# Four more chunks of a linear-attention and mixture-of-experts kernel get their y with features on partitions

## The chip, the cores and the metric

One core of one Trainium2 chip runs the whole program. The metric is device time in microseconds (us); the median of the runs of a kernel counts.

## What is computed

```python
state = f[:, :, t, :, None] * state + einsum('bhd,bhde' of k[t], v[t])   # f = sigmoid(f_logit)
y[:, :, t] = np.einsum('bhd,bhde->bhe', q[:, :, t], state)              # B 4, H 8, S 768, D 48
x = y as 3072 tokens x 384
x = (h * sigmoid(h)) @ w_out          # h = x @ w_in, 384 -> 2048 -> 384
out = one of 8 experts per token      # relu(x @ w1[e]) @ w2[e], 384 -> 1024 -> 384, times its gate
```

## The kernel before, in words

The 3072 tokens are 24 **chunks** of 128, six to a batch row. Each chunk goes through the gated linear attention, its result y goes into the first dense layer, and that layer's result is sorted by expert. All large products are made from pairs of rounded halves (hi and lo of the weights, of x and of the hidden layer), so a dense product is three matmuls. Chunks stand in groups (0 and 1; 2 and 3; 4 to 6; then threes), and a group's x has to be there when the first of its dense steps begins.

**A step** s is one pass of the loop at L1439. It makes a hidden piece `ph` of 128 features for one group (`moe_h`: nine matmuls, then tanh into `se` on ACT and the product `sg` on DVE), splits the piece into `gh` (ACT) and `gl` (DVE) in `moe_g`, and adds the piece of two steps ago to the output `px` in `moe_o`. Steps 0 to 5 serve group 0, steps 6 to 11 group 1, steps 12 to 31 take the two in turn, and from step 32 on group 2 and the others follow.

**The lists.** What else is done in the first 27 steps is written out by hand in STEPS (L38): three lists for each step, done before `moe_h`, between it and `moe_g`, and after `moe_o`. Step s is line 39 + s. All of it is pinned: on each engine, and on SP's queue of transfers, it is issued in this order, `moe_h`, `moe_g` and `moe_o` with it. The names used below: `lo`/`li` load a raw piece of a weight (SP), `co0` to `co2` and `ci0` to `ci2` join its two 32-bit words (DVE, tiles `out_cv` and `in_cv`), `ho`/`hi` round it (ACT), `Lo`/`Li` take the rest (DVE); `f`, `k`, `q`, `v` load a chunk's inputs (SP, four raw buffers for weights); `fclamp:g`, `fexp:g`, `flog:g` make the log decays of a whole group from f (DVE, ACT, ACT; the log needs another table on ACT, and `table` puts the first one back); `pl` sums them; `en`, `ep`, `kmul`, `qmul` scale k and q; `ends` and `a` bring a chunk's total decay over DRAM to `a_all` (SP); `fk`, `fq`, `kt`, `qt` turn k and q; `sc` makes the scores and `am` masks them (DVE, `mask` at L500); `past`, `own` and `pu` are the products with the state, with v, and for the next state; `st` updates the state (DVE, `carry`); `y` copies y out of PSUM (ACT); `pt`, `xh`, `xl` turn y (PE) and round it into x (ACT and DVE).

**Two forms of y.** Chunks 0 to 6 leave y with tokens on partitions: in `y_past` (L529) and `y_own` (L538) the scores are the stationary operand and 48 columns of v pass by, and `flip_y` (L630) turns y with three transposes. From chunk 7 on (YT, L104) `att4_turned` (L579) makes v and the state stationary, 64 columns of them, and lets 128 columns of scores or q pass by; y stands with features on partitions at once, in two 64-row halves of two banks, ACT copies it into `yt`, and eight transfers on SP's queue, one for each head, put its rows in place (`y<-yt`, L617). `yt` is a tile of the tag `am`, which has two buffers; a chunk's two masked score tiles need both.

Of the kernel before, what the change touches and what calls it, by code (L numbers as in the profile page):

```python
# [21 lines left out]
P = 128  # L22
# [43 lines left out]
)  # L66
KACT = 7
# [42 lines left out]
def kernel(  # L110
# [84 lines left out]
    def load_chunk(n, names, pin=lambda fn: fn):  # L195
        b, c = divmod(n, CPB)
        g, r = group_of[n]
        for nm in names:
            src = {"f": f_logit, "q": q, "k": k, "v": v}[nm]
            if nm == "v":  # L200
                tag, bufs = ("gl", GB) if n == 1 else ("in_v", 1)
                flat = att.tile([P, H * D + 16], F32, tag=tag, name=f"v_{n}", bufs=bufs)
                if n >= YT:
                    nc.gpsimd.memset(flat[:, H * D :], 0.0)
                t = flat[:, : H * D].rearrange("p (h d) -> p h d", h=H)
                loaded[nm, n] = flat
# [12 lines left out]
            loaded.setdefault((nm, n), t)
# [297 lines left out]
    def gain(n):  # L517
# [8 lines left out]
                )  # L526
        bd["pu", n] = pu[:112]

    def y_past(n):  # L529
        py, qt = y_banks(n), bd["qt", n]  # L530
        for r in range(NPR):
            for j in range(2):
                rows = slice(64 * j, 64 * j + D)
                pe.matmul(
                    py[j][:, r * D : (r + 1) * D], qt[rows, r, :], packed_state[rows, r, :D], start=r == 0, stop=False
                )

    def y_own(n):  # L538
        py, vt, a = y_banks(n), loaded["v", n], am.pop(n)
        for r in range(NPR):  # L540
            for j in range(2):
                h = 2 * r + j
                pe.matmul(
                    py[j][:, r * D : (r + 1) * D], a[j][:, r, :], vt[:, h * D : (h + 1) * D],
                    start=n % CPB == 0 and r == 0, stop=r == NPR - 1,
                )

    def y_out(n):
        y = att.tile([P, KC, P], F32, tag="y", name=f"y_{n}")
        y5 = y.rearrange("p c (r j e) -> p j c r e", j=2, e=P // H)  # L550
        for j, py in enumerate(bd.pop(("py", n))):
            ac.copy(y5[:, j], py[:, : NPR * D].rearrange("p (r e c) -> p c r e", r=NPR, c=KC))
        ysb[n] = y

    def att4(n):
        if n >= YT:
            qt = bd.pop(("qt", n))
            att4_turned(n, qt, loaded.pop(("v", n)), am.pop(n), n % CPB == 0, n % CPB == CPB - 1)
            return
# [19 lines left out]
    def att4_turned(n, qt, vt, a, first, last):  # L579
        halves_of = [use(n, 5, f"pya_{n}"), use(n, 6, f"pyb_{n}")]  # L580

        def place(r, j):
            b, c = divmod(r, 2)
            k = j ^ b
            return halves_of[b][64 * k : 64 * k + 64, c * P : (c + 1) * P]

        if not first:
            for c in range(2):
                for r in (c, c + 2):
                    for j in range(2):  # L590
                        rows = slice(64 * j, 64 * j + D)
                        pe.matmul(place(r, j), packed_state[rows, r, :], qt[rows, r, :], start=c == 0, stop=False)
        for r in range(NPR):
            for j in range(2):
                h = 2 * r + j
                pe.matmul(
                    place(r, j), vt[:, h * D : h * D + 64], a[j][:, r, :], start=first and r % 2 == 0, stop=r % 2 == 1
                )
        pu = halves_of[0][:, 2 * P : 2 * P + NPR * D]
        if not last:  # L600
            for r in range(NPR):
                for j in range(2):
                    h = 2 * r + j
                    pe.matmul(
                        pu[64 * j : 64 * j + 64, r * D : (r + 1) * D], kpads[n % 2][:, h, :],
                        vt[:, h * D : (h + 1) * D], start=True, stop=True,
                    )
        yt = att.tile([P, NPR, P], F32, tag="am", name=f"yt_{n}", bufs=2)
        for b in range(2):
            nc.scalar.copy(  # L610
                yt[:112, 2 * b : 2 * b + 2], halves_of[b][:112, : 2 * P].rearrange("p (r t) -> p r t", r=2)
            )
        y = att.tile([P, KC, P], F32, tag="y", name=f"y_{n}")
        for h in range(H):
            r, j = divmod(h, 2)
            k = j ^ r // 2
            nc.sync.dma_start(out=y[h * P // H : (h + 1) * P // H], in_=yt[64 * k : 64 * k + D, r])  # L617
        ysb[n] = y
        if not last:
            carry(n, pu[:112], first)  # L620

    def x_of(n):
        g, r = group_of[n]
# [11 lines left out]
        bd["pt", n] = pt[:, :DM].rearrange("p (c t) -> p c t", c=KC)  # L635

    def x_high(n):
        ac.copy(x_of(n)[0], bd["pt", n])

    def x_low(n):  # L640
# [1 line left out]
        ve.tensor_sub(xt[g][1][:, r], bd.pop(("pt", n)), xt[g][0][:, r].bitcast(F32))  # L642

    def att5(n):
        if n >= YT:
            xh, xl = x_of(n)
            y = ysb.pop(n)
            nc.scalar.copy(xh, y)
            nc.vector.tensor_sub(xl, y, xh.bitcast(F32))
            return  # L650
        flip_y(n)
# [753 lines left out]
    def queue(early):  # L1405
# [115 lines left out]
```

## Time and profile before

| | |
|---|---|
| median of 3 runs | 824.69 us (824.22 to 826.69) |
| the profiled execution | 826.82 us, of which the span is 825.0 us |
| PE, DVE, ACT busy | 97%, 57%, 46% of the span |
| granted TensorE clock, mean | 0.99 of 2.4 GHz |

Busy times of PE are modelled from pipelined matmuls, so a busy PE may still be one that goes at half its clock; the starts of the matmuls show its pace. The listed steps end some 126 us into the span; up to there DVE, which joins and splits the weights, is busy in most windows too. After that PE works without a gap on the dense products.

### The profile page before, as it was taken

The page shows a single profiled execution, that of the slowest core. Times are in us where ns is not written, and L with a number is a line of the kernel's source. Part 1 is how long each engine was busy: PE and PEld are TensorE (multiplying, and loading weights), DVE is VectorE, ACT ScalarE, POOL GpSimd, SP SyncE. Part 2 cuts the span into 40 slices and gives each one's busy share as a digit, 9 for nine tenths or more (in the row PEclk, how much of TensorE's full clock was granted, in tenths as well). Part 3 has the DMA queues.
Part 4 walks back from the last instruction along what each step waited for, and adds up shares of the span by engine and source line. Part 5 has one row for each costly group of instructions (what it writes and reads, how often), then busy time and mean ns, then how long its engine had stood idle before and what let it go on. Part 6 is the DMA issues. An engine that isn't in the chain of part 4 may idle for free.

```text
span 825.0 us, 15612 instructions
## 1 busy us (share of the span) xinstructions
PE 804.2 (97%) x5836; PEld 755.2 (92%) x5836; DVE 468.7 (57%) x1258; ACT 378.1 (46%) x838; POOL 61.6 (7%) x111
## 2 busy tenths in 40 slices
PE   8999999999999999999999999999999999999994
PEld 5799989999999999999999999999899999989994
DVE  7978886465556555656646556366573426345520
ACT  5564464453453453454445343354473436445520
POOL 2000000002000100100100101001200010111001
PEclk9989999999999999999999999999999999999998
DMA  9855675324343343343343322323380617644500
GB/s 211 213 130 148 156 238 175 68 40 102 87 92 80 100 97 85 93 107 78 107 97 78 106 58 52 123 61 124 123 291 23 203 48 258 221 152 161 172 17 29
DMA packets 171396, 99.11 MB, mean 120 GB/s; under 512 B 115339, under 2 KB 164923, under 8 KB 171310
## 3 DMA queue, kind: packets, MB, share of 16 engines
q1 hardware_dynamic: 166924, 87.34, 38.6%
q0 software_dynamic: 3280, 9.49, 3.1%
q10 hardware_dynamic: 1106, 1.18, 0.4%
q8 instruction: 48, 0.79, 0.4%
q14 instruction: 38, 0.31, 0.1%
HBM read 78.76 MB, written 16.33 MB: 115 GB/s over the span
## 4 chain that ended last, share of the span: by engine, by line
PE 76%; issue 8%; DVE 6%; DMA 4%; ACT 2%; POOL 1%; SPq 1%; POOLq 0%; ACTq 0%; DVEq 0%
PE ph L408 22%; PE px L408 21%; PE po L408 7%; PE p L408 7%; PE pya L408 3%; PE sc L408 3%; DMA w_raw<-in_moe_w_dram 2%; PE pyb L408 2%; PE py L408 1%; PE pl L408 1%; PE plt L413 1%; PE pq L413 1%; DVE in_cv L236 1%; PE p_r L408 1%; POOL out_dram L983 1%
## 5 line engine op out<-in xcount | busy, mean ns | idle before, releaser
L408 PE MATMUL px<-out_lo,gh 128*128 128x384 f32 x384 | 137.3, 358 | 0.0
L408 PE MATMUL px<-out_hi,gl 128*128 128x384 f32 x384 | 129.9, 338 | 0.3 <-DVE gl L236 0.2
L408 PE MATMUL px<-out_hi,gh 128*128 128x384 f32 x384 | 129.0, 336 | 0.0
L408 PE MATMUL ph<-xth,in_lo 128*128 128x384 f32 (+1 forms) x384 | 124.3, 324 | 0.8 <-DVE sg L677 0.6
L408 PE MATMUL ph<-xth,in_hi 128*128 128x384 f32 (+1 forms) x384 | 124.0, 323 | 0.0
L408 PE MATMUL ph<-xtl,in_hi 128*128 128x384 f32 (+1 forms) x384 | 122.8, 327 | 1.2 <-DVE sg L236 1.1
L677 DVE SCALAR_TENSOR_TENSOR sg<-se,ph 128x384 f32<-128x384 f32 (+1 forms) x117 | 61.9, 529 | 108.3 <-ACT se L675 107.8
L675 ACT ACTIVATE se<-ph 128x384 f32<-128x384 f32 (+1 forms) x117 | 55.1, 471 | 142.0 <-PE ph L408 139.5
L685 ACT CAST gh<-sg 128x384 fp32r<-128x384 f32 (+1 forms) x117 | 57.9, 495 | 51.8 <-DVE sg L677 49.4
L686 DVE TENSOR_TENSOR gl<-sg,gh 128x384 fp32r<-128x384 f32 (+1 forms) x117 | 62.3, 532 | 28.5 <-ACT gh L685 27.6
L408 PEld LDWEIGHTS px<-out_lo,gh 128*128 128x128 f32 x384 | 72.6, 189 | 3.1 <-issue 0.9
L408 PEld LDWEIGHTS ph<-xtl,in_hi 128*128 128x128 f32 x384 | 72.0, 189 | 3.2 <-DVE sg L236 2.1
L408 PEld LDWEIGHTS ph<-xth,in_lo 128*128 128x128 f32 x384 | 72.6, 189 | 1.6 <-DVE sg L677 1.0
L408 PEld LDWEIGHTS px<-out_hi,gl 128*128 128x128 f32 x384 | 72.6, 189 | 1.4 <-DVE gl L236 0.8
L408 PEld LDWEIGHTS ph<-xth,in_hi 128*128 128x128 f32 x384 | 72.6, 189 | 0.0
L408 PEld LDWEIGHTS px<-out_hi,gh 128*128 128x128 f32 x384 | 72.3, 188 | 0.0
L408 PE MATMUL po<-w_lo,hh 128*128 128x384 f32 (+4 forms) x184 | 62.9, 342 | 0.0
L408 PE MATMUL po<-w_hi,hl 128*128 128x384 f32 (+4 forms) x184 | 62.0, 337 | 0.2 <-DVE hl L943 0.2
L408 PE MATMUL po<-w_hi,hh 128*128 128x384 f32 (+4 forms) x184 | 61.9, 336 | 0.0
L264 DVE TENSOR_TENSOR w_lo<-w_raw,w_hi 128x384 fp32r<-128x384 f32 x104 | 52.6, 555 | 13.9 <-ACT w_hi L263 13.9
L408 PE MATMUL p<-xsl,w_hi 128*128 128x480 f32 (+6 forms) x168 | 58.4, 347 | 0.0
L408 PE MATMUL p<-xsh,w_hi 128*128 128x480 f32 (+6 forms) x168 | 58.3, 347 | 0.0
(275 smaller groups left out, 1511.8 us busy)
## 6 DMA issues: line engine op xcount, KB each, us to landing
w_raw<-in_moe_w_dram SPq DMA_DIRECT2D x64, 384.0 KB
xs<-big SPq DMA_DIRECT2D x8, 776.0 KB
in_again<-in_moe_w_in_dram SPq DMA_DIRECT2D x16, 384.0 KB
out_again<-in_moe_w_out_dram SPq DMA_DIRECT2D x16, 384.0 KB
in_raw<-in_moe_w_in_dram SPq DMA_DIRECT2D x15, 384.0 KB
xe<-xs SPq DMA_DIRECT2D x7, 776.0 KB
out_raw<-in_moe_w_out_dram SPq DMA_DIRECT2D x14, 384.0 KB
f<-in_f_logit_dram SPq DMA_DIRECT2D x24, 192.0 KB
```

Source lines behind the costliest of these rows:

```text
L236: return lambda *a, **k: tc.keep_in_program_order(fn(*a, **k))
L264: (keep(lo_engine.tensor_sub) if pin else lo_engine.tensor_sub)(lo[:, h], x, hi[:, h].bitcast(F32))
L408: ins = nc.tensor.matmul(*a, **k)
L413: ins = nc.tensor.transpose(*a, **k)
L675: ac.activation(e, ph[:, :GT], AF.Tanh, scale=0.5)
L677: ve.scalar_tensor_tensor(out=t, in0=e, scalar=1.0, in1=ph[:, :GT], op0=ALU.add, op1=ALU.mult)
L685: ac.copy(hi, t)
L686: ve.tensor_sub(lo, t, hi.bitcast(F32))
L983: ins = nc.gpsimd.indirect_dma_start(out=out[:, :], out_offset=bass.IndirectOffsetOnAxis(ap=idx[:n], axis=0), in_=o[:n], in_offset=None, b ...
```

## The change

`turned(n)` is true for chunks 2, 4, 5 and 6 as well as from 7 on. The branches of `att4_turned` move into `y_past`, `y_own` and `y_out`, and a new list entry `yd` (`y_turn`) issues the eight transfers. In the lists of those four chunks `pt` goes, `yd` stands one step after `y`, and `xh` and `xl` move one to two steps later. `fclamp:2` moves ahead in its list and `fexp:2` behind `moe_o` of the same step; `fclamp:3` moves from step 19 to step 18, and `fexp:3` to the end of step 19. The four chunks' v tiles get a memset of 16 padding columns on POOL.

```diff
-    ('co0:3 co1:3', 'co2:3 lo:6 hi:5 Li:5 st:2 fk:3 fq:3 kt:3 qt:3 a:3 fclamp:2 fexp:2', 'pt:2 xh:2 sc:3 xl:2'),
-    ('am:3 co0:4 co1:4', 'co2:4 li:7 ho:3 Lo:3', 'flog:2 table:0 lf:4 lf:5 lf:6 past:3 own:3 pu:3 y:3 v:4'),
+    ('co0:3 co1:3', 'co2:3 lo:6 hi:5 Li:5 fclamp:2 yd:2 st:2 fk:3 fq:3 kt:3 qt:3 a:3', 'sc:3 fexp:2'),
+    ('am:3 co0:4 co1:4', 'co2:4 li:7 ho:3 Lo:3 xh:2 xl:2', 'flog:2 table:0 lf:4 lf:5 lf:6 past:3 own:3 pu:3 y:3 v:4'),
...
-    ('co0:8 co1:8', 'co2:8 lo:10 hi:8 Li:8 st:4 pl:5 en:5 ep:5 kmul:5 qmul:5 k:6 q:6', ''),
-    ('ci0:9 ci1:9', 'ci2:9 li:11 ho:8 Lo:8 pt:4 xh:4 xl:4', ''),
+    ('co0:8 co1:8', 'co2:8 lo:10 hi:8 Li:8 yd:4 st:4 pl:5 en:5 ep:5 kmul:5 qmul:5 k:6 q:6', ''),
+    ('ci0:9 ci1:9', 'ci2:9 li:11 ho:8 Lo:8', ''),
...
-    ('ci0:10 ci1:10', 'ci2:10 li:12 ho:9 Lo:9 sc:5 am:5', ''),
+    ('ci0:10 ci1:10', 'ci2:10 li:12 ho:9 Lo:9 xh:4 xl:4 sc:5 am:5', ''),
...
-    ('ci0:11 ci1:11', 'ci2:11 li:13 ho:10 Lo:10 pl:6 en:6 ep:6 kmul:6 qmul:6 ends:6 f:7 f:8 f:9', ''),
-    ('co0:11 co1:11', 'co2:11 lo:13 hi:11 Li:11 pt:5 xh:5 xl:5', ''),
-    ('ci0:12 ci1:12', 'ci2:12 li:14 ho:11 Lo:11 fk:6 fq:6 kt:6 qt:6 a:6', ''),
-    ('co0:12 co1:12', 'co2:12 lo:14 hi:12 Li:12 sc:6 am:6 fclamp:3 fexp:3', ''),
+    ('ci0:11 ci1:11', 'ci2:11 li:13 ho:10 Lo:10 yd:5 pl:6 en:6 ep:6 kmul:6 qmul:6 ends:6 f:7 f:8 f:9', ''),
+    ('co0:11 co1:11', 'co2:11 lo:13 hi:11 Li:11', ''),
+    ('ci0:12 ci1:12', 'ci2:12 li:14 ho:11 Lo:11 fk:6 fq:6 kt:6 qt:6 a:6 fclamp:3', ''),
+    ('co0:12 co1:12', 'co2:12 lo:14 hi:12 Li:12 xh:5 xl:5 sc:6 am:6', 'fexp:3'),
...
-    ('ci0:14 ci1:14', 'ci2:14 ho:13 Lo:13 st:6', ''),
-    ('co0:14 co1:14', 'co2:14 hi:14 Li:14 pt:6 xh:6 xl:6', ''),
+    ('ci0:14 ci1:14', 'ci2:14 ho:13 Lo:13 yd:6 st:6', ''),
+    ('co0:14 co1:14', 'co2:14 hi:14 Li:14', ''),
...
-    ('co0:15 co1:15', 'co2:15 hi:15 Li:15', ''),
+    ('co0:15 co1:15', 'co2:15 hi:15 Li:15 xh:6 xl:6', ''),
...
-YT = 7
+TURN = (2, 4, 5, 6)
...
+    def turned(n):
+        return n > 6 or n in TURN
...
+    def place(n, r, j):
+        b, c = divmod(r, 2)
+        k = j ^ b
+        return y_banks(n)[b][64 * k : 64 * k + 64, c * P : (c + 1) * P]
...
+                if turned(n):
+                    pe.matmul(place(n, r, j), packed_state[rows, r, :], qt[rows, r, :], start=r % 2 == 0, stop=False)
...
+                if turned(n):
+                    pe.matmul(
+                        place(n, r, j), vt[:, h * D : h * D + 64], a[j][:, r, :],
+                        start=first and r % 2 == 0, stop=r % 2 == 1,
+                    )
...
+    def y_turn(n):
+        yt = ysb[n]
+        y = ysb[n] = att.tile([P, KC, P], F32, tag="y", name=f"y_{n}")
+        for h in range(H):
+            r, j = divmod(h, 2)
+            k = j ^ r // 2
+            sy.dma_start(out=y[h * P // H : (h + 1) * P // H], in_=yt[64 * k : 64 * k + D, r])
```

## Rows read from the trace of the kernel before

**Rows 1.** The page: the span, and busy time of each engine.

```profile
span 825.0 us, 15612 instructions
PE 804.2 (97%) x5836; PEld 755.2 (92%) x5836; DVE 468.7 (57%) x1258; ACT 378.1 (46%) x838; POOL 61.6 (7%) x111
```

**Rows 2.** Stretches: us; PE, PEld, DVE, ACT, POOL busy; granted clock, DMA share, GB/s.

```profile
47.40:54.00 6.60, 6.60 (x40) 6.42 (x40) 2.94 (x8) 5.77 (x10) 0.00 (x0) 0.50 0.33 89
...
71.20:74.50 3.30, 3.30 (x22) 2.90 (x18) 0.15 (x1) 1.11 (x4) 0.00 (x0) 0.50 0.52 134
```

**Rows 3.** Timeline of DVE: start, length, engine, line, operation [idle before, and its releaser].

```profile
43.67 0.43 DVE L236 TENSOR_TENSOR gl<-sg,gh 128x256 fp32r<-128x256 f32 x1 [1.53 <-ACT gh L236]
...
44.53 1.28 DVE L236 TENSOR_TENSOR am<-sc,trir 128x512 f32<-128x512 f32 x2
...
52.76 0.42 DVE L236 SCALAR_TENSOR_TENSOR sg<-se,ph 128x256 f32<-128x256 f32 x1 [3.62 <-ACT se L236]
...
74.35 0.42 DVE L236 SCALAR_TENSOR_TENSOR sg<-se,ph 128x256 f32<-128x256 f32 x1 [3.44 <-ACT se L236]
...
92.09 0.42 DVE L236 SCALAR_TENSOR_TENSOR sg<-se,ph 128x256 f32<-128x256 f32 x1 [2.05 <-ACT se L236]
...
99.70 0.42 DVE L236 TENSOR_TENSOR gl<-sg,gh 128x256 fp32r<-128x256 f32 x1
...
103.37 0.75 DVE L236 TENSOR_SCALAR f<-f 128x1152 f32<-128x1152 f32 x1
...
105.65 0.42 DVE L236 TENSOR_TENSOR gl<-sg,gh 128x256 fp32r<-128x256 f32 x1 [1.53 <-ACT gh L236]
```

**Rows 4.** The chain that ended last, in order of time: start, length, what.

```profile
123.03 1.33 PE ph L408 x9
```

**Rows 5.** Timeline of PE: chunk 4, tokens on partitions.

```profile
67.85 0.31 PE L408 MATMUL py<-state,qt 48*128 48x48 f32 x1
...
68.88 0.42 PE L408 MATMUL py<-v,am 128*128 128x48 f32 x2
...
70.79 0.82 PE L408 MATMUL py<-v,kpad 128*64 128x48 f32 x16
```

**Rows 6.** Timeline of PE: chunk 7, turned.

```profile
146.24 0.33 PE L408 MATMUL pya<-qt,state 48*64 48x128 f32 x2
...
146.84 0.66 PE L408 MATMUL pya<-am,v 128*64 128x128 f32 x8
...
147.76 0.62 PE L408 MATMUL pya<-v,kpad 128*64 128x48 f32 x16
148.31 0.44 PE L408 MATMUL pl<-lfh,trir 128*128 128x384 f32 x1
```

**Rows 7.** Timeline of SP's queue (issues), and of ACT where it waits for them.

```profile
42.13 0.66 SPq L236 DMA_DIRECT2D out_raw<-in_moe_w_out_dram  x1
...
94.16 2.86 SPq L236 DMA_DIRECT2D f<-in_f_logit_dram  x3
...
149.78 4.43 SPq L617 DMA_DIRECT2D y<-yt  x7
...
155.65 0.51 ACT L648 CAST xth<-y 128x384 fp32r<-128x384 f32 x1 [1.86 <-DMA y<-yt]
...
261.02 5.03 SPq L617 DMA_DIRECT2D y<-yt  x8
```

**Rows 8.** Timeline around a later group's f: its three loads, and the clamp that waits.

```profile
360.66 2.74 SPq L218 DMA_DIRECT2D f<-in_f_logit_dram  x3
...
366.19 0.76 DVE L380 TENSOR_SCALAR f<-f 128x1152 f32<-128x1152 f32 x1 [1.49 <-DMA f<-in_f_logit_dram]
```

**Rows 9.** Timeline of ACT in step 4: rounding, then the log between two table loads.

```profile
47.03 0.41 ACT L236 CAST gh<-sg 128x256 fp32r<-128x256 f32 x1 [2.32 <-DVE sg L236]
47.45 1.28 ACT L236 ACT_TABLE_LOAD   x1
...
51.21 0.32 ACT L236 COPY y<-py 128x192 f32<-128x192 f32 x1
```

More of the change, by code (lines that the diff above doesn't have):

```diff
@@ L202, in load_chunk @@
                 flat = att.tile([P, H * D + 16], F32, tag=tag, name=f"v_{n}", bufs=bufs)
-                if n >= YT:
+                if turned(n):
                     nc.gpsimd.memset(flat[:, H * D :], 0.0)
@@ L527, in gain @@
         bd["pu", n] = pu[:112]
+    def place(n, r, j):
+        b, c = divmod(r, 2)
+        k = j ^ b
+        return y_banks(n)[b][64 * k : 64 * k + 64, c * P : (c + 1) * P]
     def y_past(n):
-        py, qt = y_banks(n), bd["qt", n]
-        for r in range(NPR):
+        qt = bd["qt", n]
+        for i in range(NPR):
+            r = (0, 2, 1, 3)[i] if turned(n) else i
             for j in range(2):
                 rows = slice(64 * j, 64 * j + D)
-                pe.matmul(
-                    py[j][:, r * D : (r + 1) * D], qt[rows, r, :], packed_state[rows, r, :D], start=r == 0, stop=False
-                )
+                if turned(n):
+                    pe.matmul(place(n, r, j), packed_state[rows, r, :], qt[rows, r, :], start=r % 2 == 0, stop=False)
+                else:
+                    pe.matmul(
+                        y_banks(n)[j][:, r * D : (r + 1) * D], qt[rows, r, :], packed_state[rows, r, :D],
+                        start=r == 0, stop=False,
+                    )
     def y_own(n):
-        py, vt, a = y_banks(n), loaded["v", n], am.pop(n)
+        vt, a, first = loaded["v", n], am.pop(n), n % CPB == 0
         for r in range(NPR):
@@ L542, in y_own @@
                 h = 2 * r + j
[L543 to L546, printed above, removed]
-    def y_out(n):
+                if turned(n):
+                    pe.matmul(
+                        place(n, r, j), vt[:, h * D : h * D + 64], a[j][:, r, :],
+                        start=first and r % 2 == 0, stop=r % 2 == 1,
+                    )
+                else:
+                    pe.matmul(
+                        y_banks(n)[j][:, r * D : (r + 1) * D], a[j][:, r, :], vt[:, h * D : (h + 1) * D],
+                        start=first and r == 0, stop=r == NPR - 1,
+                    )
+    def y_out(n):
+        py = bd.pop(("py", n))
+        if turned(n):
+            yt = att.tile([P, NPR, P], F32, tag="am", name=f"yt_{n}", bufs=2)
+            for b in range(2):
+                ac.copy(yt[:112, 2 * b : 2 * b + 2], py[b][:112, : 2 * P].rearrange("p (r t) -> p r t", r=2))
+            ysb[n] = yt
+            return
         y = att.tile([P, KC, P], F32, tag="y", name=f"y_{n}")
         y5 = y.rearrange("p c (r j e) -> p j c r e", j=2, e=P // H)
-        for j, py in enumerate(bd.pop(("py", n))):
-            ac.copy(y5[:, j], py[:, : NPR * D].rearrange("p (r e c) -> p c r e", r=NPR, c=KC))
+        for j in range(2):
+            ac.copy(y5[:, j], py[j][:, : NPR * D].rearrange("p (r e c) -> p c r e", r=NPR, c=KC))
         ysb[n] = y
+    def y_turn(n):
[5 more added lines that the diff above has]
+            sy.dma_start(out=y[h * P // H : (h + 1) * P // H], in_=yt[64 * k : 64 * k + D, r])
     def att4(n):
[L556 to L559, printed above, removed]
         if n % CPB:
@@ L565, in att4 @@
         y_out(n)
+        if turned(n):
+            y_turn(n)
         if n % CPB < CPB - 1:
@@ L577, in carry @@
             ve.tensor_tensor(out=s, in0=s, in1=ab, op=ALU.mult)
[L579 to L620, printed above, removed]
     def x_of(n):
@@ L637, in x_high @@
     def x_high(n):
+        if turned(n):
+            bd["pt", n] = ysb.pop(n)
         ac.copy(x_of(n)[0], bd["pt", n])
@@ L644, in att5 @@
     def att5(n):
[L645 to L651, printed above, removed]
+        if not turned(n):
+            flip_y(n)
         x_high(n)
@@ L1416 @@
         sc=scores, am=mask, pu=gain, st=lambda n: carry(n, bd.pop(("pu", n)), n % CPB == 0), past=y_past, own=y_own,
-        y=y_out, pt=flip_y, xh=x_high, xl=x_low,
+        y=y_out, yd=y_turn, pt=flip_y, xh=x_high, xl=x_low,
         ends=lambda n: put_ends(n, queue(n == 0)), a=lambda n: spread_ends(n, queue(n == 0)),
```

## The prediction

> **What bounds the kernel now.** I read the page first. PE is busy for 804.2 of the 825.0 us [rows 1], so work taken off PE should count almost in full. That mean covers two stages, though, and the four chunks lie in the first, the 126 us of listed steps. So next I read the timeline of DVE there. DVE works on end for long stretches and stops only where it waits for a tanh of PE's result: 3.62 us ahead of 52.76, 3.44 ahead of 74.35, 2.05 ahead of 92.09, and 1.53 twice behind an exponential on ACT [rows 3]. The stretches between hold no gap, and each wait stands behind a chunk's products or the decays. In the listed steps, then, DVE sets the time, and PE's work on y counts only where DVE waits for it; from 123.03 on the chain is PE's alone [rows 4]. Third, the granted clock: 0.50, that is 1.2 instead of 2.4 GHz, from 47.40 to 54.00 and from 71.20 to 74.50, each time behind the thin products of a chunk in the old form (chunks 3 and 4) [rows 2].
>
> I write a shift for "later than before at the same instruction" and follow it along four instructions of DVE.
>
> **What a turned chunk saves on PE.** Chunk 4's product with the state runs from 67.85 to 68.88, 1.03 us, and that with v to 70.79, 1.91 us [rows 5]. The turned chunk 7 takes 0.60 (146.24 to 146.84) and 0.92 (to 147.76) for the same [rows 6]: 0.43 and 0.99 saved, 1.42 in all (chunk 6, first of its batch row, has the second only). The product for the next state stays. The three transposes go too. Chunks 2 and 6 save nothing that counts: DVE has no gap behind them that waits for PE, and behind chunk 6 the wait is for ACT's tables. The copies out of PSUM stay on ACT, two for a chunk. The memsets of padding on POOL, 16 columns each, come while POOL is idle, long ahead of the product; if one came late, `own` would wait for it. I price them and the copies at nothing.
>
> **Chunk 2: the transfers and the next mask.** `yd:2` stands in SP's queue behind `lo:6`, which is issued at 42.13 and takes 0.66 [rows 7]; so the first of the eight is issued at 42.8. Eight take 5.03, and the last has landed 1.44 us behind its issue (149.78 + 4.43 = 154.21, the waiting `xth` begins at 155.65) [rows 7]. The last of chunk 2 lands at 42.8 + 5.0 + 1.45 = 49.25. These transfers read `yt_2`, which holds one of the two `am` buffers, and `am:3` needs both. In the kernel before its pair runs at 44.53, ending at 45.81 [rows 3]; now the first half can run at 42.4 (the `gl` ahead no longer waits 1.53 for the exponential [rows 3]), and the second waits with all of DVE behind it until 49.25, to end at 49.9: 4.1 us later. Behind it wait `sg` of step 4 and `gh`, which began 1.22 after the mask's end (47.03), and then on ACT the two table loads with the log between them, at whose end y of chunk 3 is copied 4.18 later (51.21) [rows 9]. Both keep their distance: 49.9 + 1.22 + 4.18 = 55.3 for the copies; with two copies and a tanh (about 1.1, an estimate from the 0.32 of a copy [rows 9]) the next `sg` is at 56.4 instead of 52.76. **Shift +3.6**; of 4.1, DVE's old wait covers 0.5. PE is also held: `own:3` needs the mask, so PE stands idle for about 5 us, and I let the low clock last to about 54 as before.
> The Trainium skill's page "DMA: Bandwidth & Descriptors", section "Anatomy of one DMA", puts the fixed part of a transfer at about 2.0 us; by that the landing and the sum would be 0.6 us later. The row's 1.44 is smaller, and I keep it. `a:3` and `li:7`, queued behind `yd:2` on SP, are due a step and more later; I cost their 5 us at nothing.
>
> **Chunk 4.** DVE ran out of work at 70.91 (74.35 less 3.44) [rows 3]; at +3.6 that is 74.5. PE saves 1.42, and I expect the stretch at half clock to go, since no turned chunk of the later stage has one: half of 3.30, 1.65 [rows 2]. So the tanh is later by 3.6 - 3.07 = 0.5 at most, and `sg` of step 11 is at 74.85. **Shift +0.5**. `yd:4` delays `k:6`, `q:6` and `li:11` by 5 us; they are needed steps later, and cost nothing unless raw buffers run short. `xl:4` moves from step 12 to 14, both in one gapless stretch of DVE: nothing.
>
> **Chunk 5.** DVE ran out at 90.04 (92.09 less 2.05), now at 90.55. PE has its 1.42 and the transposes of chunk 4 less to do, so the tanh is there first; DVE's wait of 2.05 goes. `sg` of step 16 is at 90.55: **shift -1.55**.
>
> **The clamp of group 3.** Before the change the three loads of f are issued from 94.16 [rows 7] and the clamp runs at 103.37 [rows 3]. Now `yd:5` stands ahead of them on SP, 5.0 us, and the clamp one step sooner, ahead of `gl` of step 18 (99.70) [rows 3]. From the first issue to a clamp that waits for the three took 5.53 where a weight load went in between [rows 8]; I take 5.0, as here the queue is empty. Counted from DVE's own progress, f is there at 94.16 + 5.0 + 5.0 = 104.2, so the clamp ends at 104.95 and `gl` follows there. From that `gl` to the old clamp DVE had 3.67 of work (99.70 to 103.37); with `xl:5`, now also in this part (about 0.5, an estimate by the 0.42 of a `gl` of 256 columns), `gl` of step 19 comes at 109.1 instead of 105.65: +3.45. In this figure the old wait of 1.53 behind the exponential is already gone. **Shift -1.55 + 3.45 = +1.9.** From here to 123 the tables of `flog:3` on ACT and DVE's chain are as before. `yd:6` and the move of `xl:6` end inside the same steps: nothing, or a few tenths less.
>
> **Sum**: +3.6 - 3.1 - 2.05 + 3.45 = +1.9 us. Against the profiled execution's 826.82 that is 828.7; that execution is 2.1 above the median of the runs, 824.69, and the same shift gives **826.6**.
>
> **Bounds of what no row shows.** The landing of `yd:2` is at best hidden (0) and at worst follows a full queue, 1 us more than I took; the landing of f costs between -1.53 (in time) and +4.0 (5.53 instead of 5.0). The low clock behind the hole on PE costs from 0 to 1.65 more, and chunk 4's may stay (1.65). I take values near the late ends of the first two, since the same transfers, in the same order on the same queue, were waited for in most turned chunks.
>
> **Rivals.**
> *One wait is hidden.* If the mask finds its buffer free, the shifts are 0, -3.0, -5.0 and -1.55: 823.1. If instead f is there in time, they end at -1.55 - 1.53 = -3.1: 821.6. For it: the loads of f had 9.2 before the old clamp (94.16 to 103.37). Against: both waits are on DVE, whose stretches have no gap. 0.16 for the two.
> *Both are hidden*: -5.0 - 1.5 = -6.5, 818.2. It needs transfers that are issued much faster here than in all later chunks: 0.14, which leaves room for an order of the queues that I read wrongly.
> *Slower: the clock.* Behind the hole of about 5 us on PE the clock stays at 1.2 GHz for one stretch more (3.3 us, 1.65 lost), and the one of chunk 4 comes all the same (1.65). It is decided at chunk 4: if the granted clock is low at its products, the shift there is +0.5 + 3.3 = +3.8, then +1.75, then +5.2: 829.9. For it speaks that chunk 3, old form, follows the hole directly. Against it: chunks 2, 5 and 6 went through old-form products at full clock. 0.22.
> The skill's page "TensorE: Matmul & The Clock Gate", section "HAM oscillation — how this bites in real kernels", has such a case: matmul groups that wait for transfers start at the low clock again each time. No row before shows a hole of this length inside these steps.
>
> **How the numbers follow.** The forecast, both waits and the full clock at chunk 4, has 0.48, with a range of its own from 825.0 to 828.5. About 0.3% (2.5 us) is what a measurement can tell from no change: 822.2 and 827.2 are the marks. Of the forecast's 0.48, 0.32 lies between the marks and 0.16 above. Faster: both hidden 0.14 and half of the third case 0.08, 0.22. Same: 0.32 + 0.08 = 0.40. Slower: 0.16 + 0.22 = 0.38. The range from 821.0 to 830.0 leaves out the case with both hidden and little else.
>
> **What would show it.** DVE's second mask of chunk 3 waits some 6 us for `y<-yt`; the clamp of 128x1152 in step 18 waits some 5 us for f; DVE's waits of 3.44 and 2.05 shrink to under 0.5; the clock is 1.00 around chunk 4's products, which last 2.1 us with the state's. If the mask does not wait, or the clamp finds its f, the forecast is wrong on the fast side; a stretch at 0.50 at chunk 4 makes it wrong on the slow side.

## The result and the profile after

The change makes the kernel slower: 831.37 us median (828.66 to 835.23, six runs) against 825.10 for the kernel before in the same comparison, a ratio of 1.007 (95%: 1.0049 to 1.0091). Twelve more runs of the changed kernel gave 830.79 (828.47 to 832.65) against 826.64, 1.0048 (1.0031 to 1.0065); I take the cost as 4 to 6 us. The forecast was 826.6, +1.9, with "no change" as the likeliest outcome. The sum pointed the right way, but the kernel is slower by more than twice as much, and 831.37 lies above the range, which ended at 830.0.

The profiled execution took 835.23 us. Its page (the span; busy time, share and instructions of each engine):

```profile
span 833.5 us, 15659 instructions
PE 801.5 (96%) x5824; PEld 751.8 (90%) x5824; DVE 467.9 (56%) x1258; ACT 378.5 (45%) x838; POOL 62.0 (7%) x115
```

Against [rows 1] PE is busy for 2.7 us less and the span is 8.5 us longer, so what was added is not work of PE but waiting. The timeline of DVE shows where (start, length, engine, line, operation, [idle before, releaser]):

```profile
18.85 0.36 DVE L239 TENSOR_TENSOR state<-py,a_all 112x192 f32<-112x192 f32 x1 [2.04 <-DMA a_all<-ends]
...
54.55 0.69 DVE L239 TENSOR_TENSOR am<-sc,trir 128x512 f32<-128x512 f32 x1 [6.93 <-DMA y<-yt]
...
62.21 0.42 DVE L239 SCALAR_TENSOR_TENSOR sg<-se,ph 128x256 f32<-128x256 f32 x1 [3.18 <-ACT se L239]
...
80.94 0.42 DVE L239 SCALAR_TENSOR_TENSOR sg<-se,ph 128x256 f32<-128x256 f32 x1 [0.57 <-ACT se L239]
...
96.54 0.41 DVE L239 SCALAR_TENSOR_TENSOR sg<-se,ph 128x256 f32<-128x256 f32 x1
...
108.93 0.76 DVE L239 TENSOR_SCALAR f<-f 128x1152 f32<-128x1152 f32 x1 [5.16 <-DMA f<-in_f_logit_dram]
```

The last five answer to [rows 3] line by line: a new wait of 6.93 for chunk 2's transfers, 3.18 where 3.62 was, 0.57 where 3.44 was, none where 2.05 was, and a new wait of 5.16 at the clamp. These are the places that the prediction named. The first row, at 18.85, lies ahead of every turned chunk, and DVE is already 4.54 us late at its first `sg` (32.61 against 28.07 before). That part has to be counted apart.

SP's queue has both causes (start, time in issue, queue, operation):

```profile
46.26 0.65 SPq L239 DMA_DIRECT2D out_raw<-in_moe_w_out_dram  x1
47.01 5.91 SPq L239 DMA_DIRECT2D y<-yt  x8
...
98.09 5.72 SPq L239 DMA_DIRECT2D y<-yt  x8
103.91 0.39 SPq L239 DMA_DIRECT2D ends<-ep  x1
104.40 1.77 SPq L239 DMA_DIRECT2D f<-in_f_logit_dram  x3
```

Eight transfers take 5.7 to 5.9 us to issue where the row of before had 5.03 [rows 7]; the mask begins 1.63 after the eighth (54.55 less 52.92), and f is issued only when chunk 5's eight are out.

**One table for all profiles.** As the opening differs from run to run, I give the shift against the first profile of before at the first `sg`, and then how much later (or sooner) than that the same instruction comes. Steps 5, 11 and 16 are the `sg` behind chunks 3, 4 and 5; "19" is `gl` of step 19, behind the clamp; "142" is the `sg` that stood at 142.51 before. The last column is the measured ratio of the times to those of the kernel before, run beside it; "x under the changed kernel" in the text below compares medians with the 830.79 of its twelve runs, and the kernel before has 826.46, 826.64 and 826.69 in the three comparisons concerned.

| kernel | first sg | 5 | 11 | 16 | 19 | 142 | ratio (95%) |
|---|---|---|---|---|---|---|---|
| forecast | 0 | +3.6 | +0.5 | -1.55 | +1.9 | +1.9 | 1.0023 |
| changed | +4.54 | +4.91 | +2.05 | -0.09 | +3.55 | +3.65 | 1.007 (1.0049 to 1.0091) |
| changed again (e5) | -0.32 | +4.80 | +1.86 | -0.27 | +4.45 | +4.55 | 1.0048 (1.0031 to 1.0065) |
| before again (e12) | +1.48 | -0.68 | -0.90 | -0.90 | -0.91 | -0.88 | 1.0017 (0.9993 to 1.0041) |
| e1 chunk 2 old | +0.66 | -0.91 | -3.84 | -5.96 | -1.85 | -1.74 | 0.9955 (0.9933 to 0.9977) |
| e2 f before y | +3.12 | +5.29 | +2.89 | +0.77 | +0.98 | +1.09 | 1.0009 (0.999 to 1.0027) |
| e3 both | +4.45 | -2.24 | -5.14 | -7.27 | -6.25 | -5.90 | 0.992 (0.9894 to 0.9947) |
| e4 clamps alone | +0.22 | -2.23 | -3.68 | -3.68 | -5.08 | -5.08 | 0.9971 (0.9947 to 0.9996) |
| e6 yt apart | +0.07 | +2.58 | +1.00 | -1.13 | +2.80 | +2.94 | 1.0059 (1.0037 to 1.0081) |
| e7 and xh later | +0.58 | -0.93 | -1.18 | -3.31 | +1.22 | +1.36 | 1.001 (0.999 to 1.003) |
| e8 f early | +3.55 | -1.45 | -4.13 | -6.27 | -2.76 | -2.66 | 0.9949 (0.9929 to 0.9968) |
| e9 waits moved | +5.01 | -2.25 | -5.17 | -7.30 | -7.77 | -2.94 | 0.9987 (0.9966 to 1.0008) |
| e10 chunk 4 alone | +3.21 | -0.67 | -3.60 | -4.66 | -4.66 | -4.65 | 0.9944 (0.9924 to 0.9964) |
| e11 chunk 6 old | +2.32 | -0.85 | -3.78 | -5.91 | -4.86 | -4.83 | 0.9934 (0.9911 to 0.9957) |

Before and before again differ by 0.9 in these columns, so that is about what one profile can tell.

### The profile page after: what moved, and what is told of

It is laid out like the page before. It is cut to its first block, busy times and chain, and to the rows that moved or that the text cites. A ratio compares the mean times of both kernels' runs of the same rounds, so it can differ in the third digit from the quotient of the medians.

```text
span 833.5 us, 15659 instructions
## 1 busy us (share of the span) xinstructions
PE 801.5 (96%) x5824; PEld 751.8 (90%) x5824; DVE 467.9 (56%) x1258; ACT 378.5 (45%) x838; POOL 62.0 (7%) x115
## 3 DMA queue, kind: packets, MB, share of 16 engines
q10 hardware_dynamic: 1106, 1.18, 0.4%
## 4 chain that ended last, share of the span: by engine, by line
PE 78%; issue 7%; DMA 5%; DVE 5%; ACT 1%; POOL 1%; SPq 1%; POOLq 0%; DVEq 0%; ACTq 0%
PE px L411 22%; PE ph L411 22%; PE po L411 7%; PE p L411 7%; PE py L411 4%; PE sc L411 2%; DMA w_raw<-in_moe_w_dram 2%; PE pyb L411 2%; PE pl L411 1%; PE pq L416 1%; PE plt L416 1%; PE pk L416 1%; POOL out_dram L969 1%; PE p_r L411 1%; PE po_r L411 1%
```

## The experiments

**The changed kernel once more (e5).**

> The changed kernel once more, unaltered. The first comparison had six runs of it, and its profile was 4.5 us late before any turned chunk. Theory: that lateness is a draw that each kernel's runs make (the profiles of the other kernels have 0.2 to 4.5 us of it), and the change itself is worth +3.6 us: the lowest times of the two kernels lie 3.5 to 4.5 us apart, and the shift of this profile, counted from the first sg, is 3.6 within 0.4, whatever its opening does. Rival: the change causes the late opening; then this profile has it again (the first sg 3 us or more later than before, the clock at 0.50 from about 20 to 28) and none of the runs is under 829.

The first `sg` comes 0.32 us sooner than before, with the clock at 1.00 from 20 to 28 us, and the two new waits are there all the same (its timeline of DVE):

```profile
49.57 0.69 DVE L239 TENSOR_TENSOR am<-sc,trir 128x512 f32<-128x512 f32 x1 [6.81 <-DMA y<-yt]
...
75.89 0.42 DVE L239 SCALAR_TENSOR_TENSOR sg<-se,ph 128x256 f32<-128x256 f32 x1 [0.51 <-ACT se L239]
...
104.97 0.76 DVE L239 TENSOR_SCALAR f<-f 128x1152 f32<-128x1152 f32 x1 [6.25 <-DMA f<-in_f_logit_dram]
```

So the change does not bring the late opening with it each time. The lowest times of these runs are 4.7 apart (828.47 and 823.75), and the shift at 142 is 4.55, both a little above the bounds of 4.5 and 4.0 that I had set. By the profile's end 1.4 us of the 4.55 is gone again: the span is 827.8 against 825.0, +3.1 counted in the same way (the first profile of the changed kernel: +4.0). Where it goes stays open.

**Undo chunk 2 (e1)**, against the changed kernel, as all that follows where nothing else is said:

```diff
-    ('co0:3 co1:3', 'co2:3 lo:6 hi:5 Li:5 fclamp:2 yd:2 st:2 fk:3 fq:3 kt:3 qt:3 a:3', 'sc:3 fexp:2'),
-    ('am:3 co0:4 co1:4', 'co2:4 li:7 ho:3 Lo:3 xh:2 xl:2', 'flog:2 table:0 lf:4 lf:5 lf:6 past:3 own:3 pu:3 y:3 v:4'),
+    ('co0:3 co1:3', 'co2:3 lo:6 hi:5 Li:5 fclamp:2 st:2 fk:3 fq:3 kt:3 qt:3 a:3', 'pt:2 xh:2 sc:3 xl:2 fexp:2'),
+    ('am:3 co0:4 co1:4', 'co2:4 li:7 ho:3 Lo:3', 'flog:2 table:0 lf:4 lf:5 lf:6 past:3 own:3 pu:3 y:3 v:4'),
...
-TURN = (2, 4, 5, 6)
+TURN = (4, 5, 6)
```

> The changed kernel with chunk 2 in its old form again (its own product, transposes and list entries as before; chunks 4 to 6 stay turned, the clamps stay where the change put them). Theory: the mask of chunk 3 finds its buffer free, so the 6.93 us wait of DVE and the hole of PE behind it are gone; DVE's shift at sg of step 5 falls from +4.9 to between 0 and -1.5, and those of the later terms (-2.9 at chunk 4, -2.1 at chunk 5, +3.6 at the clamp) stay. Time 4.9 to 6.4 below the changed kernel, that is 1.3 to 2.8 below the kernel before. Rival A, the opening: the changed kernel's profile is 4.5 us late already before step 4; if that comes from the change (its memsets on POOL are the only new work there), three of four memsets are still here and the time stays above the kernel before by 0.5 or more. Rival B, the turned form itself: if a turned chunk costs by its transfers wherever it stands, undoing one of four gives back a quarter, 1.6 us.

823.79 us, 7.0 under the changed kernel where 4.9 to 6.4 was expected; the table has 5.4 to 6.3 at 142. The mask runs at 43.59 without a wait. Rival A falls (the time is below the kernel before), and so does B: one chunk out of four gives back more than the whole loss.

**f ahead of chunk 5's transfers (e2), and both edits (e3).**

```diff
-    ('ci0:11 ci1:11', 'ci2:11 li:13 ho:10 Lo:10 yd:5 pl:6 en:6 ep:6 kmul:6 qmul:6 ends:6 f:7 f:8 f:9', ''),
+    ('ci0:11 ci1:11', 'ci2:11 li:13 ho:10 Lo:10 pl:6 en:6 ep:6 kmul:6 qmul:6 ends:6 f:7 f:8 f:9 yd:5', ''),
```

> The changed kernel with the eight transfers of chunk 5 behind the three loads of f on SP's queue, not ahead of them. Theory: the clamp of group 3 waited 5.16 us only for these loads; with f issued 5.7 us sooner its wait falls under 1 us, gl of step 19 comes 4 to 5 us sooner, and the time is 3.5 to 5 below the changed kernel, 1.3 to 2.8 above the kernel before. Rival: the place of the clamp, one step sooner, is what costs; then the loads are late anyway, the wait stays at 2 us or more and the time falls by less than 3. In this order xh of chunk 5 gets its y 1.8 us later; it stands two steps on, and should not wait.

> Both edits of the two runs ahead of this one together: chunk 2 in its old form, and the loads of f ahead of chunk 5's transfers. Theory: the two waits add, so this takes off the sum of the two runs' savings, within 1 us: 8.4 to 11.4 below the changed kernel, 2 to 5 below the kernel before (chunk 4's 2.9 and chunk 5's 2.1 are left as gains, and the 1.5 of the late exponential). Rival: the later wait absorbs what the earlier one cost (a DVE that comes sooner waits longer for f), and the sum falls short by 2 us or more; or the opening costs as it did, and the time is not below the kernel before.

With f first, e2's clamp waits 0.93 instead of 5.16 to 6.25, in the step to which the change had moved it (its timeline of DVE):

```profile
104.14 0.76 DVE L239 TENSOR_SCALAR f<-f 128x1152 f32<-128x1152 f32 x1 [0.93 <-DMA f<-in_f_logit_dram]
...
108.08 0.56 DVE L239 TENSOR_TENSOR xtl<-y,xth 128x384 fp32r<-128x384 f32 x1 [0.71 <-ACT xth L239]
```

The second row is the small price: y of chunk 5 is later, and its `xtl` waits. The time is 827.22, 3.6 under the changed kernel. Both edits give 820.67, 10.1 under it, where the two alone gave 7.0 and 3.6: they add. At 0.992 (0.9894 to 0.9947), some 6.6 us below the kernel before by the ratio and 5.8 by the medians, this has the lowest ratio of all kernels here; 2 to 5 was expected. A part of the 5.90 in its profile is the clock: behind chunk 3 it stays at 1.00, where e1 has a stretch at 0.50, and step 5 comes 1.33 sooner than in e1.

**The clamps alone (e4)**, against the kernel before:

```diff
-    ('co0:3 co1:3', 'co2:3 lo:6 hi:5 Li:5 st:2 fk:3 fq:3 kt:3 qt:3 a:3 fclamp:2 fexp:2', 'pt:2 xh:2 sc:3 xl:2'),
+    ('co0:3 co1:3', 'co2:3 lo:6 hi:5 Li:5 fclamp:2 st:2 fk:3 fq:3 kt:3 qt:3 a:3', 'pt:2 xh:2 sc:3 xl:2 fexp:2'),
...
-    ('ci0:12 ci1:12', 'ci2:12 li:14 ho:11 Lo:11 fk:6 fq:6 kt:6 qt:6 a:6', ''),
-    ('co0:12 co1:12', 'co2:12 lo:14 hi:12 Li:12 sc:6 am:6 fclamp:3 fexp:3', ''),
+    ('ci0:12 ci1:12', 'ci2:12 li:14 ho:11 Lo:11 fk:6 fq:6 kt:6 qt:6 a:6 fclamp:3', ''),
+    ('co0:12 co1:12', 'co2:12 lo:14 hi:12 Li:12 sc:6 am:6', 'fexp:3'),
```

> The kernel before with the two clamps and their exponentials moved as in the change, and no chunk turned. Theory: without chunk 5's transfers the loads of f are out at 94.2 and land near 99.7, where the clamp now stands, so it waits under 0.5 us; the two waits of 1.53 us on the exponential go, the first into the 3.62 us wait that follows at sg of step 5. Time 0.5 to 2 below the kernel before. Rival: the clamp's new place alone makes it wait for f; then the time is 1 us or more above the kernel before.

0.9971, a gain of 2.4 us (0.3 to 4.4), where 0.5 to 2 was expected. The profile shows more, 5.08 at 142, but only 1.40 of that comes at the clamp, between steps 16 and 19; 1.45 comes at step 11, where the clock stays at 1.00 here, and the rest ahead of step 5. The clamp waits for nothing, and the two waits of 1.53 are gone. So the clamp's new place is a gain; it became a loss only by the transfers put ahead of f. This profile shows something more (stretches: PE, PEld, DVE, ACT, POOL busy; granted clock, DMA share, GB/s):

```profile
48.00:56.00 8.00, 7.94 (x65) 7.19 (x65) 5.18 (x13) 5.62 (x13) 0.00 (x0) 1.00 0.40 110
66.00:72.00 6.00, 6.00 (x62) 5.57 (x61) 3.99 (x10) 2.47 (x8) 0.00 (x0) 1.00 0.52 151
```

Chunks 3 and 4 are in the old form here, and the clock is 1.00 behind both; DVE's wait ahead of `sg` of step 11 is 1.97, not 3.44.

**Chunk 4 alone (e10), against the kernel before, and that kernel again (e12).**

```diff
+TURN = (4,)
...
-    ('co0:8 co1:8', 'co2:8 lo:10 hi:8 Li:8 st:4 pl:5 en:5 ep:5 kmul:5 qmul:5 k:6 q:6', ''),
-    ('ci0:9 ci1:9', 'ci2:9 li:11 ho:8 Lo:8 pt:4 xh:4 xl:4', ''),
+    ('co0:8 co1:8', 'co2:8 lo:10 hi:8 Li:8 yd:4 st:4 pl:5 en:5 ep:5 kmul:5 qmul:5 k:6 q:6', ''),
+    ('ci0:9 ci1:9', 'ci2:9 li:11 ho:8 Lo:8', ''),
...
-    ('ci0:10 ci1:10', 'ci2:10 li:12 ho:9 Lo:9 sc:5 am:5', ''),
+    ('ci0:10 ci1:10', 'ci2:10 li:12 ho:9 Lo:9 xh:4 xl:4 sc:5 am:5', ''),
```

> The kernel before with chunk 4 alone turned; clamps and every other chunk as before. Theory: DVE's wait ahead of sg of step 11 shrinks from 3.44 to 0.5 where the kernel before falls to half clock there, and from 1.97 to 0.5 where it does not (as in the run with the clamps alone); nothing waits for its transfers. Time 1.5 to 2.9 below the kernel before. Rival: what DVE gains is lost at the next wait that does not move (the tanh behind chunk 5's products, 2.05 us, in its old form), and the time is the same within 0.5 us.

> The kernel before, unaltered, for a second profile of it. Two stretches at half clock stood in its first profile (47.4 to 54.0 and 71.2 to 74.5), and neither in the run with the clamps alone, which has the same chunks. Theory: the low clock behind chunk 4 is a draw of the run, not a property of the old form; in about half of the profiles it is absent, and then DVE's wait ahead of sg of step 11 is about 2 us and not 3.44. Rival: it belongs to the old form with these lists, and both stretches are here again.

e10 gains 2.93 between steps 5 and 11, the wait being 0.50, and 1.06 more at step 16 (its timeline of DVE):

```profile
73.96 0.42 DVE L239 SCALAR_TENSOR_TENSOR sg<-se,ph 128x256 f32<-128x256 f32 x1 [0.50 <-ACT se L239]
...
90.64 0.42 DVE L239 SCALAR_TENSOR_TENSOR sg<-se,ph 128x256 f32<-128x256 f32 x1 [0.98 <-ACT se L239]
```

The 2.05 of before has become 0.98 although chunk 5 is in its old form: chunk 4's transposes no longer stand on PE ahead of chunk 5's products. The time, 0.9944 (0.9924 to 0.9964), is 3.0 to 6.3 us lower, more than the 2.9 I had as the upper end. Of the 4.65 in the table, 0.67 is there at step 5 already, ahead of chunk 4, as in the kernel before when it is run again; some 4.0 belong to the turned chunk, and nothing of it is given back. In e12 the stretch behind chunk 4 is again partly at 1.2 GHz (second row, 0.64 as a mean; the wait is 3.21, not the 2 that I had expected), and behind chunk 3, the first row, it is not. These are stretches of e12, with the columns of e4's:

```profile
48.00:56.00 8.00, 6.32 (x60) 5.95 (x60) 4.99 (x14) 6.10 (x10) 0.00 (x0) 1.00 0.36 83
72.00:76.00 4.00, 4.00 (x20) 3.47 (x19) 1.07 (x3) 1.93 (x6) 0.00 (x0) 0.64 0.46 117
```

So behind chunk 3 the low clock is a matter of the run. Behind chunk 4 it came in both profiles of the kernel before and not in e4, which has the same chunk some 2 us sooner; with three profiles, what decides there stays open. In all eleven profiles with chunk 4 turned the clock is 1.00 from 64 to 82 us.

**The mask's buffer (e6), and then the cast (e7).**

```diff
-            yt = att.tile([P, NPR, P], F32, tag="am", name=f"yt_{n}", bufs=2)
...
+                if n == 2:
+                    t = att.tile([P, ROW], F32, tag="x2", name=f"yt_{n}_{b}", bufs=5)
+                    half = t[:, : 2 * P].rearrange("p (r t) -> p r t", r=2)
```

> The changed kernel with chunk 2's turned product in two buffers of its own (those of x2, unused until much later) and not in one of the two that the mask of chunk 3 needs; all four chunks turned, the lists as in the change. Theory: the mask does not wait any more, but the cast xth of chunk 2 on ACT waits for the last transfer to the same moment (it waited 6.54 us for y beside the mask), and gh of step 4 and the two table loads stand behind it on ACT. So the wait moves from DVE's mask to ACT's cast: the chain comes 1 to 2 us sooner (the second half of the mask, sg and gh no longer follow each other behind the transfer), time 1 to 2 below the changed kernel. Rival, the buffer as the prediction had it: the mask was the only thing that waited, and all of its 4.9 us come back.

The mask's pair runs at 42.53 and waits no more. ACT and then DVE wait in its place (ACT's and DVE's timeline):

```profile
49.96 0.51 ACT L239 CAST xth<-y 128x384 fp32r<-128x384 f32 x1 [6.46 <-DMA y<-yt]
50.79 1.28 ACT L239 ACT_TABLE_LOAD   x1
```

```profile
50.50 0.56 DVE L239 TENSOR_TENSOR xtl<-y,xth 128x384 fp32r<-128x384 f32 x1 [4.56 <-ACT xth L239]
```

The trace gives 2.2 of the 4.8 back at step 5; the time, 830.76, shows nothing of it, where 1 to 2 us was expected. Either way the rival, that the mask's buffer alone was the cause, is out. In e7 `xh` and `xl` follow the two table loads:

```diff
-    ('am:3 co0:4 co1:4', 'co2:4 li:7 ho:3 Lo:3 xh:2 xl:2', 'flog:2 table:0 lf:4 lf:5 lf:6 past:3 own:3 pu:3 y:3 v:4'),
+    ('am:3 co0:4 co1:4', 'co2:4 li:7 ho:3 Lo:3', 'flog:2 table:0 xh:2 xl:2 lf:4 lf:5 lf:6 past:3 own:3 pu:3 y:3 v:4'),
```

> As the run ahead of it, and in addition xh and xl of chunk 2 stand behind the two table loads of step 4, ahead of lf. Theory: the transfer's end is then hidden from both engines, and sg of step 5 comes within 0.6 us of where it is with chunk 2 in the old form (0.9 sooner than before, counted from the first sg); time 5 to 6 below the changed kernel, that is within 1 us of the run with chunk 2 in the old form, so that turning chunk 2 is worth nothing in itself. Rival: turning chunk 2 takes its three transposes off PE ahead of chunk 3 and is worth 1 us or more; or the clock falls all the same and costs 1.5 or more.

At step 5 e7 is where e1 is (-0.93 and -0.91), as forecast, but in part by luck: e1 goes through a stretch at half clock ahead of it, from some 49.5, and e7's begins only about 1 us ahead of it. Against e3 and e9, which have chunk 2 in its old form and the full clock there (-2.24 and -2.25), e7 is 1.3 us late. ACT still waits 0.61 for the transfer, and then comes a third holder: there is one buffer `y`, and chunk 3's copy into it waits 0.68 until chunk 2's `xl` is done. PE waits for that copy with its transposes, 3.21 in all, where e12, with both chunks in the old form and the full clock, has 1.68 (timelines of ACT and of PE).

```profile
51.55 0.32 ACT L239 COPY y<-py 128x192 f32<-128x192 f32 x1 [0.68 <-DVE xtl L239]
```

```profile
52.14 0.90 PE L416 MATMUL pt<-ident,y 128*128 128x128 f32 x3 [3.21 <-ACT y L239]
```

Behind this hole the clock is 0.50 from 52 to 58, and at step 11 e7 stands 2.7 us behind e1. The rival of a low clock took place, and the time is 3.2 above e1. Chunk 2's turned form costs through each thing that its y holds on to.

**f four steps earlier (e8)**, chunk 2 being in its old form as in e1:

```diff
-    ('ci0:9 ci1:9', 'ci2:9 li:11 ho:8 Lo:8', ''),
+    ('ci0:9 ci1:9', 'ci2:9 li:11 ho:8 Lo:8 f:7 f:8 f:9', ''),
...
-    ('ci0:11 ci1:11', 'ci2:11 li:13 ho:10 Lo:10 yd:5 pl:6 en:6 ep:6 kmul:6 qmul:6 ends:6 f:7 f:8 f:9', ''),
+    ('ci0:11 ci1:11', 'ci2:11 li:13 ho:10 Lo:10 yd:5 pl:6 en:6 ep:6 kmul:6 qmul:6 ends:6', ''),
```

> Chunk 2 in its old form and the three loads of f four steps sooner, at the end of step 12, so that chunk 5's transfers are again where the change has them. Theory: the clamp's wait (0.92 us in the run with both edits undone) and the wait of xtl for chunk 5's y (1.52 there) both go; the time is 1.5 to 2.5 below that run, 7 to 9 below the kernel before. Rival: the loads of f take bandwidth from the loads of weights at step 12, and a wait for li or lo appears there; then no gain on that run, or a loss.

It failed: 0.9949, 2.0 us above e3 by the medians instead of 1.5 to 2.5 below it. The clamp waits for nothing, as forecast, but SP stood still from 83.4 to 89.46 at the loads of f, whose only buffer is read until chunk 6's sums (88.62 to 89.43), with the weights queued behind (its timelines of SP and of DVE):

```profile
82.66 0.77 SPq L239 DMA_DIRECT2D in_raw<-in_moe_w_in_dram  x1
89.46 1.79 SPq L239 DMA_DIRECT2D f<-in_f_logit_dram  x3
91.36 0.83 SPq L239 DMA_DIRECT2D out_raw<-in_moe_w_out_dram  x1
```

```profile
97.03 0.36 DVE L239 TENSOR_SCALAR out_cv<-out_raw 128x384 uint32<-128x384 uint32 x1 [5.04 <-DMA out_raw<-in_moe_w_out_dram]
```

The rival's wait is there, but from a blocked queue and not from bandwidth.

**Two small waits moved (e9), chunk 6 undone (e11).** Both start from e3. e9 puts `fclamp:3` first in step 19 and `xh:5 xl:5` into step 20:

```diff
-    ('ci0:12 ci1:12', 'ci2:12 li:14 ho:11 Lo:11 fk:6 fq:6 kt:6 qt:6 a:6 fclamp:3', ''),
-    ('co0:12 co1:12', 'co2:12 lo:14 hi:12 Li:12 xh:5 xl:5 sc:6 am:6', 'fexp:3'),
-    ('ci0:13 ci1:13', 'ci2:13 li:15 ho:12 Lo:12', 'flog:3 table:0'),
+    ('ci0:12 ci1:12', 'ci2:12 li:14 ho:11 Lo:11 fk:6 fq:6 kt:6 qt:6 a:6', ''),
+    ('co0:12 co1:12', 'fclamp:3 co2:12 lo:14 hi:12 Li:12 sc:6 am:6', 'fexp:3'),
+    ('ci0:13 ci1:13', 'ci2:13 li:15 ho:12 Lo:12 xh:5 xl:5', 'flog:3 table:0'),
```

e11 gives chunk 6 its old form and list entries:

```diff
-    ('ci0:14 ci1:14', 'ci2:14 ho:13 Lo:13 yd:6 st:6', ''),
-    ('co0:14 co1:14', 'co2:14 hi:14 Li:14', ''),
+    ('ci0:14 ci1:14', 'ci2:14 ho:13 Lo:13 st:6', ''),
+    ('co0:14 co1:14', 'co2:14 hi:14 Li:14 pt:6 xh:6 xl:6', ''),
...
-    ('co0:15 co1:15', 'co2:15 hi:15 Li:15 xh:6 xl:6', ''),
+    ('co0:15 co1:15', 'co2:15 hi:15 Li:15', ''),
...
-TURN = (4, 5, 6)
+TURN = (4, 5)
```

> The kernel with both edits undone (chunk 2 old, f ahead of chunk 5's transfers), and two of its remaining waits moved: the clamp of group 3 stands first in step 19, not last in step 18 (it waited 0.92 us for f), and xh, xl of chunk 5 stand in step 20, not 19 (xtl waited 1.52). Theory: both waits go; gl of step 19 comes 1.5 to 2.4 us sooner, and the time is as much below that run, 8 to 9 below the kernel before. Rival: the exponential that follows the clamp becomes the wait for gl of step 19, as in the kernel before (1.53), and half or more of it is given back; then it is within 1 us of that run.

> The kernel with both edits undone, and chunk 6 in its old form as well (with its transposes; its list entries as before). The prediction put turning chunk 6 at nothing: its wait is for ACT's tables. Theory: within 1 us of the run with both edits undone. Rival: PE's 0.99 us and the three transposes count after all, and this is 1 to 2 us slower; or the eight transfers of chunk 6 cost, and it is 1 us or more faster.

e9 gains its 1.5 at step 19 and loses 4.8 behind it; its time, 824.94, is 4.3 above e3's. Its SP issues chunk 6's eight transfers at 116.41, behind a load of a weight that alone takes 3.26 (1.72 in e3), and what e3 hides is now waited for (its timelines of ACT and of DVE):

```profile
123.34 0.51 ACT L239 CAST xth<-y 128x384 fp32r<-128x384 f32 x1 [4.83 <-DMA y<-yt]
```

```profile
123.89 0.56 DVE L239 TENSOR_TENSOR xtl<-y,xth 128x384 fp32r<-128x384 f32 x1 [2.65 <-ACT xth L239]
```

Behind this wait the clock falls as well, to 0.50 from 126 to 128 (1.00 in e3). Why that load's issue took longer, no run shows. e11 is at 821.76, 1.1 above e3 with overlapping intervals, and between step 19 and 142 it moves by 0.03, e3 by 0.35: turning chunk 6 changes nothing that can be told.

## Why the prediction was wrong

**The places were right.** The mask waits for `y<-yt`, the clamp for f, the waits of 3.44 and 2.05 go, and the clock is 1.00 around chunk 4's products. The turned chunk 4 takes exactly what chunk 7 did [rows 6]: 0.60 and 0.92 (77.02, 77.62, 78.54).

**Chunk 2, the term that was mis-sized: +3.6 forecast, +4.9 and +4.8 measured.** Counted from the first `sg`, the first of the eight was issued at 42.47 (42.8 forecast), the eight took 5.91 (5.03), and the landing 1.63 (1.45): the mask's second half is 0.76 later than 49.25. Another 0.5 comes behind it: from that mask to `sg` of step 5 took 7.66, 7.15 was forecast. It lies in the last piece, from the copy of y to `sg`: 1.57 (60.64 to 62.21), where I had estimated 1.1 although [rows 9] and [rows 3] give 1.55 for it (51.21 to 52.76); with the full clock there, e12 has 0.86. The hole on PE, and the stretches there, of the changed kernel's first profile (columns as in e4's):

```profile
55.29 0.66 PE L411 MATMUL pyb<-v,am 128*128 128x48 f32 x2 [5.61 <-DVE am L239]
```

```profile
48.00:52.00 4.00, 1.54 (x19) 1.27 (x18) 0.00 (x0) 0.00 (x0) 0.00 (x0) 1.00 0.44 134
52.00:54.00 2.00, 0.00 (x0) 0.00 (x0) 0.00 (x0) 0.00 (x0) 0.00 (x0) 0.67 0.14 37
54.00:62.00 8.00, 6.71 (x42) 6.53 (x43) 4.42 (x10) 5.39 (x8) 0.11 (x1) 0.50 0.31 75
```

PE's hole lasts 5.61 us, and the clock stays low to 62, that is 57.5 counted from the first `sg`, not to about 54. I had taken the issue time from chunks after the listed steps, and there from a quick one: the trace of before also has a slow one, on SP's queue,

```profile
240.66 5.94 SPq L617 DMA_DIRECT2D y<-yt  x8
```

and in the lists every set of eight takes 5.3 to 6.6. The ~2.0 us of the Trainium skill's page "DMA: Bandwidth & Descriptors", section "Anatomy of one DMA", would have put the landing 0.4 too late; but that section describes transfers issued by GpSimd and these are SP's, so it gave no price for them, and the row decides. The Trainium skill's page "TensorE: Matmul & The Clock Gate", section "HAM oscillation — how this bites in real kernels", describes matmuls that start at the low clock after a wait for a transfer; the trace agrees, 0.50 behind this hole. That the wait for chunk 2's transfers would move, not end, once the mask is free (e6, e7) was not in the prediction.

**Chunk 4, -3.1 forecast: -2.86 and -2.94, right in size.** That half of it is the clock and half PE's own work fits e4, where the old form at the full clock has a wait of 1.97 in place of 3.44, and the turned form has 0.57; no run changes the clock by itself.

**Chunk 5, -2.05 forecast: -2.14 and -2.13, right.** e10 shows that 1.06 of it belongs to chunk 4's transposes.

**The clamp, +3.45 forecast: +3.64 and +4.72.** Mechanism and place were right; the eight transfers ahead of f took 5.72 and 6.22 in place of 5.0, and from f's first issue to the clamp it took 4.53 and 5.12, where 5.0 was forecast.

**Chunk 6 at nothing:** right (e11), though e9 shows how little covers its transfers. **Chunk 2's products at nothing:** not shown by itself, as no run has the turned products without the transfers; e7, no faster than e1, doesn't speak against it.

**The sum.** The terms give +3.65 and +4.55 at 142, not +1.9, and +4.0 and +3.1 at the end of the span. The first six runs have some 2 us above this (831.37 against 825.10 is 6.3), which the twelve runs don't repeat (4.2); as only one of the six was profiled, what the others lost stays open. So the rivals with a hidden wait were wrong, and the clock rival's price (+5.2) was near, but not its reason: the clock did stay low longer behind the hole, but chunk 4 ran at the full clock. The step that failed is thus the price of chunk 2's wait, +3.6 where +4.9 and +4.8 were measured, and in the second profile that of the clamp, +3.45 where it was +4.72: both were worked out with 5.0 us for eight issues on SP's queue, from a quick set, and 5.7 to 6.2 was measured, although the prediction says that it takes values near the late ends. The slower side was left only as far as +5.3.

## What to carry to other kernels

A wait goes with whatever still holds the late data: freeing one buffer here moved the wait to the next engine, and a part of it then to the next buffer, so follow all readers and all later writers before a transfer is put into a tight stretch. On an in-order queue, ask of each new issue what stands behind it and who waits for that; swapping two entries was worth 3.6 us. And a form that is cheaper on one engine pays where another engine waits for it: of the four chunks, chunk 4, turned alone, gave some 4 us in the trace, chunk 6 nothing that can be told, and chunk 2 a loss.

## What was not expected of the hardware

The same kernel's opening comes at two paces. In seven of the fourteen profiles (both of the kernel before, e5, e1, e4, e6, e7) the granted clock is 1.00 from 20 to 26 us and the first `sg` is -0.3 to +1.5 us from the first one seen; in six (the changed kernel's first, e2, e3, e8, e9, e10) it is at 0.50 there and the first `sg` is 3.1 to 5.0 later; e11 lies between (+2.3). The stretch from 20 to 28 of the changed kernel's first profile, of e5, and of the first of before:

```profile
20.00:28.00 8.00, 8.00 (x51) 7.01 (x51) 3.05 (x8) 3.27 (x7) 0.00 (x0) 0.50 0.57 174
```

```profile
20.00:28.00 8.00, 7.09 (x60) 5.57 (x60) 6.33 (x15) 5.43 (x12) 0.00 (x0) 1.00 0.73 204
```

```profile
20.00:28.00 8.00, 7.08 (x61) 5.53 (x60) 6.33 (x15) 5.51 (x12) 0.00 (x0) 1.00 0.66 189
```

The listed order of the work there is the same in all. On POOL it is not: in the three profiles with none of the four chunks turned (both of before, e4) it clears `big`, a row that is sent out much later, at 5.0 us; with one or more turned these two memsets stand behind the last of the new ones (at 94.85 in the changed kernel), and with chunk 2 turned its padding is cleared at some 18 us. As e1, e5, e6 and e7 have the quick opening with `big` late as well, that does not decide it. In the changed kernel's first profile the wait of 2.04 for `a_all` stands ahead of it; in e10 the same instruction waits 0.74, for ACT, and the clock falls as well. What sets it off stays open. The changed kernel has shown both paces; the three profiles with none of the four turned show only the quicker one, and three are too few to say that the slower one never comes there. The difference between the paces is as large as the effect that was to be predicted, so a single pair of profiles would have given 8.5 us for a change that costs some 4 to 6.
